# Sparse attention, a dense layer and routed experts on one core: the second batch's attention rearranged, the first weight transfer moved, sums scaled on another engine

## The chip, the cores and the metric

One core of one Trainium2 chip runs the whole program. The metric is the time of one execution in device microseconds (us); lower is better. The engines are TensorE (PE in the rows; PEld is its weight load), VectorE (DVE), ScalarE (ACT), GpSimd (POOL) and SyncE (SP), which here issues the transfers. Each engine runs its own list of instructions in a fixed order, and waits at an instruction until what it needs is there.

## What is computed

The reference, cut to what matters:

```python
# 4 batches, 8 heads, 576 positions, head size 64
scores = scale * q @ k^T            # heads 0-3: the last 32 positions; heads 4-7: every 32nd position
attn   = exp(scores - max);  attn = attn / (sum(attn) + 1e-9)
x      = attn @ v                   # 2304 tokens x 512
h      = x @ w_in                   # 512 -> 2048
g      = where(h >= 1, h, where(h <= -1, 0, (h + 1)**2 / 4))
x      = g @ w_out                  # 2048 -> 512, written to the output
# second layer: tokens with x @ w_skip > 0 go to one of 8 experts:
out    = x + gate * (relu(x @ w1[e]) @ w2[e])
```

## The kernel before

The 2304 tokens are cut into blocks of 512 (the last one 256). For each block the dense layer takes 16 steps. A step of `gemm1` (line 450) multiplies the tokens by 128 columns of `w_in` in 12 matmuls into the bank `ph`; VectorE and ScalarE make `g` of it in four instructions (lines 468 to 471: VectorE, ScalarE, VectorE, ScalarE), and GpSimd makes its low half. `gemm2` (line 475) runs three steps behind and adds 12 matmuls into the four banks `po`. Numbers are held as two fp16 halves (high and low), hence three products each.

The weights come as fp64 and are turned into fp16 halves by `load_w` (line 108): one transfer of 1 MB, six VectorE instructions (lines 128 to 130, twice) through the bank `tp`, two on ScalarE (134, 135), one on GpSimd (136). There are 16 such loads, i0 to i7 of `w_in` and o0 to o7 of `w_out`; their staging tiles have three buffers. Load i0 serves steps 0 and 1, o0 the second layer of the same steps, and so on.

Attention works on head pairs (`hp` 0 to 3) and two groups of tiles (`gi` 0 and 1). `scores` (line 191) writes the mask (line 196) and the products q k (line 204) into the bank `sc`. `softmax` (line 209) takes the maximum (220), the exponentials (by ScalarE for group 1, line 224; else 227 to 229), scales the sum (line 225 on ScalarE for group 1, line 230 on VectorE for group 0), takes the reciprocal (231), and GpSimd multiplies (232). `values` (line 236) multiplies by v into the bank `pv`, and `to_x` (line 254) writes the tokens `xr`, which `gemm1` reads. All attention instructions of batch b have to be done before the block that holds its tokens can run: block 1 needs batch 1.

Batch 0 has its own routine, `attention32` (line 276), which transposes on TensorE. The others use `attention` (line 325), which is a generator: head pair by head pair it splits v (`vn`, lines 336 to 341), scores both groups, turns the probabilities with a transposing transfer (`pT`, line 356, one buffer per group), and multiplies by v. For batch 1 the scores and the products with v share the one bank `sc`. `Filler` (line 519) hands out the generator's pieces between the steps: batch 1 over the first 13 steps, the weights over 13 steps, batch 2 over steps 16 to 25.

A scheduler then sets the order on each engine; `after(a, b)` only tells it that a stands behind b. Transfers are issued by SyncE in its order: those of batch 0 first (`load_qkv`, four head pairs), then the first weights.

Of the kernel before, what the change touches and what calls it, by code (L numbers as in the profile page):

```python
# [8 lines left out]
F32 = mybir.dt.float32  # L9
F16 = mybir.dt.float16  # L10
# [3 lines left out]
AF = mybir.ActivationFunctionType  # L14
ALU = mybir.AluOpType
# [5 lines left out]
def kernel(ctx: ExitStack, tc: tile.TileContext, q, k, v, w_in, w_out, w_skip, w_gate, w1, w2, out):  # L21
    nc = tc.nc
    B, S, D = 4, 576, 64
# [167 lines left out]
    def scores(b, hp, gi, qkv, sc):  # L191

        g0, g1 = GROUPS[gi]
        kw, mask = (96, mloc) if hp < 2 else (72, mstr)
        nt = g1 - g0
        nc.tensor.matmul(  # L196
            sc[:, : nt * kw], identb, mask[:, g0:g1, :].rearrange("p n c -> p (n c)"), start=True, stop=False
        )
        for n in range(g0, g1):
            k0 = n * (64 if hp < 2 else 72)  # L200
            t = n - g0
            for j in range(2):
                js = slice(j * D, (j + 1) * D)
                mm = nc.tensor.matmul(  # L204
                    sc[js, t * kw : (t + 1) * kw], qkv[0][js, n, :], qkv[1][js, k0 : k0 + kw], start=False, stop=n == g1 - 1
                )
        return mm

    def softmax(b, hp, gi, sc, by_act):

        g0, g1 = GROUPS[gi]
        kw = 96 if hp < 2 else 72
        nt = g1 - g0
        nm = f"{b}_{hp}_{gi}"
        scv = sc[:, : nt * kw].rearrange("p (n c) -> p n c", n=nt)
        sm = att.tile([P, nt, kw], F32, tag="sm", name=f"sm_{nm}", bufs=3)
        st = att.tile([P, 3, 5], F32, tag="st", name=f"st_{nm}", bufs=4)
        mx, su, ri = (st[:, e, :nt] for e in range(3))
        wide_k = lambda x: x.unsqueeze(2).to_broadcast([P, nt, kw])
        red = nc.vector.tensor_reduce(mx, scv, AX.X, ALU.max, negate=by_act)  # L220
        if by_act:
            nc.scalar.mul(mx, mx, SCL)
            for t in range(nt):
                nc.scalar.activation(sm[:, t], scv[:, t], AF.Exp, bias=mx[:, t : t + 1], scale=SCL, accum_out=su[:, t : t + 1])  # L224
            nc.scalar.activation(su, su, AF.Copy, bias=1.0e-9 / XS, scale=1.0 / XS)
        else:
            nc.vector.tensor_tensor(sm, scv, wide_k(mx), ALU.subtract)
            nc.scalar.activation(sm, sm, AF.Exp, scale=SCL)
            nc.vector.reduce_sum(su, sm, axis=AX.X)
            nc.vector.tensor_scalar(su, su, 1.0e-9, 1.0 / XS, ALU.add, ALU.mult)  # L230
        nc.vector.reciprocal(ri, su)  # L231
        nc.gpsimd.tensor_tensor(sm, sm, wide_k(ri), ALU.mult)  # L232
        marks["red", b, hp, gi] = red
        return sm
# [41 lines left out]
    def attention32(b):  # L276

        units = [(hp, gi) for hp in range(4) for gi in range(2)]
        held = {}

        def scored(hp, gi):
            i = 2 * hp + gi
            pool, tag = (ps_s, "sc") if i % 2 else (ps_v, "pv")
            sc = pool.tile([P, 512], F32, tag=tag, name=f"sc_{b}_{hp}_{gi}")
            held["mm"] = scores(b, hp, gi, held[hp], sc)
            held[hp, gi] = softmax(b, hp, gi, sc, gi == 1)

        def turned(hp, gi):
            g0, g1 = GROUPS[gi]
            kw = 96 if hp < 2 else 72  # L290
            sm = held[hp, gi]
            pT = att.tile([96, 5, P], F32, tag="pT", name=f"pT_{b}_{hp}_{gi}", bufs=2)
            for c0, c1, tag in ((0, 3, "po0"), (3, 5, "po1")) if gi == 0 else ((0, 4, "po2"),):
                pp = ps_o.tile([P, 512], F32, tag=tag, name=f"pp_{b}_{hp}_{gi}_{c0}")
                if c0 == 0:
                    keep_warm(16 if hp == 0 else 4, pp, held["mm"])
                for t in range(c0, c1):
                    nc.tensor.transpose(pp[:kw, (t - c0) * P : (t - c0 + 1) * P], sm[:, t], ident)  # L298
                nc.scalar.copy(pT[:kw, c0:c1], pp[:kw, : (c1 - c0) * P].rearrange("p (t r) -> p t r", r=P))
            held[hp, gi] = pT  # L300

        def valued(hp, gi):
            kw = 96 if hp < 2 else 72
            pv = ps_h.tile([P, 512], F32, tag="ph", name=f"pv_{b}_{hp}_{gi}")
            v32 = held[hp][2]

            def pairs(n, j):
                at = 0 if n < GROUPS[0][1] else 1
                return [(v32[:kw, n, j, :], held[hp, at][:kw, n - GROUPS[at][0], j * D : (j + 1) * D])]

            values(hp, gi, pv, pairs)
            to_x(pv, b, hp, gi, 1.0)

        for hp in range(4):
            held[hp] = load_qkv(b, hp)
        for i in range(len(units) + 2):
            if i >= 2:
                valued(*units[i - 2])
            if 1 <= i <= len(units):
                turned(*units[i - 1])  # L320
            if i < len(units):
                scored(*units[i])
            yield

    def attention(b):

        nxt = load_qkv(b, 0)
        for hp in range(4):
            kw = 96 if hp < 2 else 72
            nv = 96 if hp < 2 else 80  # L330
            qkv, nxt = nxt, load_qkv(b, hp + 1) if hp < 3 else None
            vn = att.tile([96, 2, NTL, 2, D], F16, tag="vn", name=f"vn_{b}_{hp}", bufs=1)
            v32 = qkv[2].rearrange("p n h d -> p (n h d)")
            vh, vl = (vn[:nv, e].rearrange("p n h d -> p (n h d)") for e in range(2))
            if b == 1:
                nc.scalar.activation(v32, v32, AF.Copy, scale=XS)
                nc.scalar.activation(vh, v32, AF.Copy)
                nc.gpsimd.tensor_tensor(vl, v32, vh, ALU.subtract)
            else:
                nc.scalar.activation(vh, v32, AF.Copy, scale=XS)  # L340
                nc.vector.scalar_tensor_tensor(vl, v32, XS, vh, ALU.mult, ALU.subtract)
            pTs = []
            yield
            for gi in range(2):
                g0, g1 = GROUPS[gi]
                nt = g1 - g0
                nm = f"{b}_{hp}_{gi}"
                sc = bank(f"sc_{nm}")
                scores(b, hp, gi, qkv, sc)
                sm = softmax(b, hp, gi, sc, gi == 1)  # L350
                pn = p_b[gi][:, : 2 * nt * P].rearrange("p (e t c) -> p e t c", e=2, t=nt)
                pnh, pnl = (pn[:, e, :, :kw] for e in range(2))
                nc.scalar.activation(pnh, sm, AF.Copy)  # L353
                nc.gpsimd.tensor_tensor(pnl, sm, pnh, ALU.subtract)  # L354
                pT = att.tile([P, 2, nt, P], F16, tag=f"pT{gi}", name=f"pT_{nm}", bufs=1)
                nc.sync.dma_start_transpose(pT.rearrange("p e t r -> p (e t) r"), pn.rearrange("p e t c -> p (e t c)"))
                pTs.append(pT)
                yield
            for gi in range(2):
                if b == 1:  # L360
                    pv = ps_s.tile([P, 512], F32, tag="sc", name=f"pv_{b}_{hp}_{gi}")
                else:
                    pv = ps_v.tile([P, 512], F32, tag="pv", name=f"pv_{b}_{hp}_{gi}")

                def pairs(n, j):
                    at = 0 if n < GROUPS[0][1] else 1
                    r = [pTs[at][:kw, e, n - GROUPS[at][0], j * D : (j + 1) * D] for e in range(2)]
                    l = [vn[:kw, e, n, j, :] for e in range(2)]
                    return [(l[0], r[0]), (l[0], r[1]), (l[1], r[0])]

                values(hp, gi, pv, pairs)
                to_x(pv, b, hp, gi, 1.0 / XS)
                yield

    def spread(t, x2):
# [74 lines left out]
    def gemm1(n, fs):  # L450
# [4 lines left out]
        for i, f in enumerate(fs):  # L455
            step = 0
            for cc in range(NCC):
                for we, xe in ((0, 0), (0, 1), (1, 0)):
                    nc.tensor.matmul(  # L459
                        ph[:, i * nt : (i + 1) * nt], w_in_s[:, we, cc, f * P : (f + 1) * P],  # L460
                        xr[:, xe, cc, t0 % XR : t0 % XR + nt], start=step == 0, stop=step == 11,
                    )
# [5 lines left out]
        nc.vector.tensor_scalar(uu, h, XS * WS, -XS * WS, ALU.min, ALU.max)  # L468
        nc.scalar.activation(uu, uu, AF.Square, bias=half, scale=0.5 * GS ** 0.5 / (XS * WS))  # L469
        nc.vector.scalar_tensor_tensor(uu, h, GS / (XS * WS), uu, ALU.mult, ALU.max)  # L470
        nc.scalar.activation(gh, uu, AF.Copy)  # L471
        nc.gpsimd.tensor_tensor(gl, uu, gh, ALU.subtract)  # L472
        gs[n, fs[0]] = g

# [64 lines left out]
            for f in fillers:  # L539
                f.upto(t + 1)  # L540

    NA = 4 * (1 + 2 * 2)
    att_b = [attention32(0)] + [attention(b) for b in range(1, B)]

    pairs_w = [("i", 0), ("i", 1)]
# [8 lines left out]
    marks["early"] = True  # L554
    keep_warm(48, ps_v.tile([P, 512], F32, tag="pv", name="idle"))
    for i, _ in enumerate(att_b[0]):
        if i >= 7 and i - 7 < 2:
            after(next(ws), marks["red", 0, 3, i - 7])
    marks["early"] = False
    next(ws)  # L560
    NW = 13
    fw = Filler(ws, NW, 0, NW)
    f1 = Filler(att_b[1], NA, 0, 13)
    f2 = Filler(att_b[2], NA, 16, 25)
    f3 = Filler(att_b[3], NA, 32, 45)
    wide[0] = False
# [301 lines left out]
```

## Time and profile before

| | us |
|---|---|
| three timed runs | 508.18, 506.29, 503.13; median 506.29 |
| the profiled execution: its time, and its span | 505.59, 503.8 |
| TensorE busy in the span | 463.7 |
| mean granted TensorE clock, share of full speed | 0.966 |

The span is from the first to the last instruction; 1.8 us lie around it. Busy time of TensorE counts overlapping matmuls once. A digit in the slices of the profile's page stands for 12.6 us.

### The profile page before, as it was taken

The page shows a single profiled execution, that of the slowest core. Times are in us where ns is not written, and L with a number is a line of the kernel's source. Part 1 is how long each engine was busy: PE and PEld are TensorE (multiplying, and loading weights), DVE is VectorE, ACT ScalarE, POOL GpSimd, SP SyncE. Part 2 cuts the span into 40 slices and gives each one's busy share as a digit, 9 for nine tenths or more (in the row PEclk, how much of TensorE's full clock was granted, in tenths as well). Part 3 has the DMA queues.
Part 4 walks back from the last instruction along what each step waited for, and adds up shares of the span by engine and source line. Part 5 has one row for each costly group of instructions (what it writes and reads, how often), then busy time and mean ns, then how long its engine had stood idle before and what let it go on. Part 6 is the DMA issues. An engine that isn't in the chain of part 4 may idle for free.

```text
span 503.8 us, 9766 instructions
## 1 busy us (share of the span) xinstructions
PE 463.7 (92%) x3836; PEld 246.3 (49%) x3836; DVE 282.2 (56%) x597; ACT 244.0 (48%) x505; POOL 198.6 (39%) x188
## 2 busy tenths in 40 slices
PE   8767899999965999999999999999999999989990
PEld 7653344444433545544445444544444444558750
DVE  4597999999333555436345553632363466565411
ACT  2674776766553655443236534342432355564210
POOL 4325577776620653421435323262113411121330
PEclk9978899999985999999999999999999999999997
DMA  8968777589157363440009112021250245635001
GB/s 226 313 206 267 238 195 243 154 256 269 29 132 191 81 135 73 94 105 1 2 21 194 27 23 47 1 44 26 66 103 1 85 168 167 174 120 128 2 2 50
DMA packets 69513, 58.72 MB, mean 117 GB/s; under 512 B 49226, under 2 KB 53322, under 8 KB 69456
## 3 DMA queue, kind: packets, MB, share of 16 engines
q1 hardware_dynamic: 68848, 57.96, 42.1%
q8 instruction: 32, 0.52, 0.4%
q14 instruction: 25, 0.20, 0.1%
q0 software_dynamic: 608, 0.03, 0.1%
HBM read 41.93 MB, written 5.03 MB: 93 GB/s over the span
## 4 chain that ended last, share of the span: by engine, by line
PE 74%; DMA 12%; DVE 6%; ACT 3%; SPq 1%; issue 1%; POOL 0%; POOLq 0%; DVEq 0%; ACTq 0%
PE ph L459 32%; PE po L483 32%; DMA esta<-in_moe_w_dram 5%; PE sc L204 3%; DMA v<-in_v_dram 3%; PE pv L252 3%; DMA k<-in_k_dram 2%; DMA pT<-p_b 1%; DVE w1sa L634 1%; ACT w1sa L633 1%; DVE w2sa L634 1%; PE sc L196 1%; PE eha L163 1%; PE pya L163 1%; PE pr L163 1%
## 5 line engine op out<-in xcount | busy, mean ns | idle before, releaser
L459 PE MATMUL ph<-xr,w_in_s 128*128 128x512 f16 (+1 forms) x960 | 206.2, 362 | 8.3 <-DVE uu L470 7.7
L483 PE MATMUL po<-w_out_s,g 128*128 128x512 f16 x864 | 201.0, 379 | 0.0
L472 POOL TENSOR_TENSOR g<-uu,g 128x512 f16<-128x512 f32 x72 | 84.5, 1174 | 168.4 <-ACT g L471 154.7
L459 PEld LDWEIGHTS <-w_in_s 128*128 128x128 f16 x960 | 91.9, 99 | 100.7 <-issue 11.4
L483 PEld LDWEIGHTS <-g 128*128 128x128 f16 x864 | 83.5, 98 | 97.3
L469 ACT ACTIVATE uu<-uu,half 128x512 f32<-128x512 f32 x72 | 51.7, 718 | 83.4 <-DVE uu L468 82.9
L468 DVE TENSOR_SCALAR uu<-ph 128x512 f32<-128x512 f32 x72 | 49.3, 685 | 49.0 <-PE ph L459 47.7
L470 DVE SCALAR_TENSOR_TENSOR uu<-ph,uu 128x512 f32<-128x512 f32 x72 | 49.5, 688 | 32.1 <-ACT uu L469 31.9
L471 ACT ACTIVATE g<-uu 128x512 f16<-128x512 f32 x72 | 45.1, 626 | 42.0 <-DVE uu L470 40.4
L232 POOL TENSOR_TENSOR sm<-sm,st 128x384 f32<-128x384 f32 (+3 forms) x32 | 26.2, 820 | 65.9 <-DVE st L231 49.6
L204 PE MATMUL sc<-k,q 64*64 64x96 f32 (+1 forms) x576 | 30.2, 246 | 3.0 <-DMA k<-in_k_dram 3.0
L204 PEld LDWEIGHTS sc<-k,q 64*64 64x64 f32 x576 | 24.2, 138 | 14.6 <-issue 14.0
L274 DVE SCALAR_TENSOR_TENSOR xr<-pv,xr 128x288 f16<-128x288 f32 (+5 forms) x38 | 15.1, 403 | 27.4 <-ACT xr L273 27.4
L220 DVE TENSOR_REDUCE st<-sc 128x5 f32<-128x480 f32 (+3 forms) x32 | 17.4, 546 | 21.0 <-PE sc L204 20.7
L354 POOL TENSOR_TENSOR p_b<-sm,p_b 128x480 f16<-128x480 f32 (+3 forms) x24 | 22.6, 941 | 14.6 <-ACT p_b L353 13.4
L273 ACT ACTIVATE xr<-pv 128x288 f16<-128x288 f32 (+5 forms) x38 | 13.8, 364 | 28.1 <-PE pv L252 27.2
L252 PE MATMUL pv<-pT,vn 96*64 96x64 f16 (+2 forms) x684 | 16.6, 200 | 9.8 <-DMA pT<-p_b 8.0
L252 PEld LDWEIGHTS <-vn 72*64 72x64 f16 (+1 forms) x684 | 13.7, 116 | 19.0 <-issue 17.2
L432 POOL DMA_INDIRECT lst<-ent,si x16 | 16.0, 997 | 14.9 <-DMA lst<-ent,si 13.4
L224 ACT ACTIVATE sm<-sc,st 128x96 f32<-128x96 f32 (+1 forms) x64 | 20.3, 330 | 2.6 <-PE pp L298 2.1
L136 POOL TENSOR_TENSOR w_in_s<-tvi,w_in_s 128x1024 f16<-128x1024 f32 x8 | 17.1, 2132 | 6.1 <-ACT w_in_s L135 4.3
L136 POOL TENSOR_TENSOR w_out_s<-tvo,w_out_s 128x1024 f16<-128x1024 f32 x8 | 17.1, 2133 | 4.0 <-ACT w_out_s L135 2.9
(141 smaller groups left out, 413.8 us busy)
## 6 DMA issues: line engine op xcount, KB each, us to landing
wi<-in_moe_w_in_dram SPq DMA_DIRECT2D x8, 1024.0 KB, 5.7
wo<-in_moe_w_out_dram SPq DMA_DIRECT2D x8, 1024.0 KB, 5.3
esta<-in_moe_w_dram SPq DMA_DIRECT2D x16, 512.0 KB, 3.6
q<-in_q_dram SPq DMA_DIRECT2D x16, 288.0 KB, 5.2
out_dram<-x SPq DMA_DIRECT2D x18, 256.0 KB, 2.1
v<-in_v_dram SPq DMA_DIRECT2D x8, 432.0 KB, 7.6
v<-in_v_dram SPq DMA_DIRECT2D x8, 360.0 KB, 6.6
k<-in_k_dram SPq DMA_DIRECT2D x8, 324.0 KB, 5.6
```

What stands on the lines that cost most here:

```text
L136: nc.gpsimd.tensor_tensor(dst[1], tvf, dst[0], ALU.subtract)
L204: mm = nc.tensor.matmul(sc[js, t * kw : (t + 1) * kw], qkv[0][js, n, :], qkv[1][js, k0 : k0 + kw], start=False, stop=n == g1 - 1)
L232: nc.gpsimd.tensor_tensor(sm, sm, wide_k(ri), ALU.mult)
L252: nc.tensor.matmul(oo, l, r, start=i == 0, stop=i == len(todo) - 1)
L354: nc.gpsimd.tensor_tensor(pnl, sm, pnh, ALU.subtract)
L459: nc.tensor.matmul(ph[:, i * nt : (i + 1) * nt], w_in_s[:, we, cc, f * P : (f + 1) * P], xr[:, xe, cc, t0 % XR : t0 % XR + nt], start=step ...
L468: nc.vector.tensor_scalar(uu, h, XS * WS, -XS * WS, ALU.min, ALU.max)
L469: nc.scalar.activation(uu, uu, AF.Square, bias=half, scale=0.5 * GS ** 0.5 / (XS * WS))
L470: nc.vector.scalar_tensor_tensor(uu, h, GS / (XS * WS), uu, ALU.mult, ALU.max)
L471: nc.scalar.activation(gh, uu, AF.Copy)
L472: nc.gpsimd.tensor_tensor(gl, uu, gh, ALU.subtract)
L483: nc.tensor.matmul(pos[n][s], g[:, ge, i * nt + s * P : i * nt + (s + 1) * P], w_out_s[:, we, f, :], start=f == 0 and si == 0, stop=f == N ...
```

## The change

The scaling of the sums, line 230 on VectorE, becomes an instruction on ScalarE for both groups. The four buffers of the transposed probabilities get one name and size for batch 0 and the others. In batch 0's routine the first weight load stands ahead of the loads of head pair 3. `attention` becomes a pipeline: the loads run two head pairs ahead, the scores of head pair i stand ahead of the products with v of head pair i-1, and v is split after them; `pT` has four buffers. For batch 1, the products with v of group 1 use the bank `pv`, in which the weights' `tp` also lies; the scores stand behind the last `gemm1` matmul issued so far, and the first scaling of v behind the last `g`. Batch 1 is handed out over the first 10 steps, in 22 pieces instead of 20.

```diff
@@ scores
-        nc.tensor.matmul(
+        m0 = nc.tensor.matmul(
             sc[:, : nt * kw], identb, mask[:, g0:g1, :].rearrange("p n c -> p (n c)"), start=True, stop=False
         )
+        if b == 1:
+            after(m0, marks["gm"])
@@ softmax
-            nc.scalar.activation(su, su, AF.Copy, bias=1.0e-9 / XS, scale=1.0 / XS)
         else:
             nc.vector.tensor_tensor(sm, scv, wide_k(mx), ALU.subtract)
             nc.scalar.activation(sm, sm, AF.Exp, scale=SCL)
             nc.vector.reduce_sum(su, sm, axis=AX.X)
-            nc.vector.tensor_scalar(su, su, 1.0e-9, 1.0 / XS, ALU.add, ALU.mult)
-        nc.vector.reciprocal(ri, su)
+        nc.scalar.activation(su, su, AF.Copy, bias=1.0e-9 / XS, scale=1.0 / XS)
+        marks["rec", b, hp, gi] = nc.vector.reciprocal(ri, su)
@@ attention32
-            pT = att.tile([96, 5, P], F32, tag="pT", name=f"pT_{b}_{hp}_{gi}", bufs=2)
+            pT = att.tile([P, 10 * P], F16, tag="pT", name=f"pT_{b}_{hp}_{gi}", bufs=4)
+            pT = pT.bitcast(F32).rearrange("p (t r) -> p t r", t=5)[:96]
         for hp in range(4):
+            if hp == 3:
+                first_w = next(ws)
             held[hp] = load_qkv(b, hp)
         for i in range(len(units) + 2):
+            if i == 6:
+                after(first_w, marks["red", b, 2, 1])
@@ attention
-        nxt = load_qkv(b, 0)
-        for hp in range(4):
+        held = []
+        for hp in range(2):
+            held.append(load_qkv(b, hp))
+            yield
+        parts, turned = {}, {}
+
+        def scored(hp, gi):
...
+            pT = att.tile([P, 10 * P], F16, tag="pT", name=f"pT_{nm}", bufs=4)[:, : 2 * nt * P]
...
+        def split(hp):
...
             if b == 1:
-                nc.scalar.activation(v32, v32, AF.Copy, scale=XS)
+                after(nc.scalar.activation(v32, v32, AF.Copy, scale=XS), marks["ga"])
...
+        def valued(hp, gi):
+            kw = 96 if hp < 2 else 72
+            if b == 1 and gi == 0:
+                pv = ps_s.tile([P, 512], F32, tag="sc", name=f"pv_{b}_{hp}_{gi}")
+            else:
+                pv = ps_v.tile([P, 512], F32, tag="pv", name=f"pv_{b}_{hp}_{gi}")
...
+        for i in range(5):
+            if i < 2:
+                held.append(load_qkv(b, i + 2))
+            if i < 4:
+                for gi in range(2):
+                    scored(i, gi)
+                    yield
+            if i > 0:
+                for gi in range(2):
+                    valued(i - 1, gi)
+                    yield
+            if i < 4:
+                split(i)
                 yield
@@ gemm1
-                    nc.tensor.matmul(
+                    marks["gm"] = nc.tensor.matmul(
...
-        nc.scalar.activation(gh, uu, AF.Copy)
+        marks["ga"] = nc.scalar.activation(gh, uu, AF.Copy)
@@ the whole
-    NA = 4 * (1 + 2 * 2)
+    NA = 2 + 4 * (1 + 2 * 2)
     for i, _ in enumerate(att_b[0]):
-        if i >= 7 and i - 7 < 2:
-            after(next(ws), marks["red", 0, 3, i - 7])
+        if i == 8:
+            after(next(ws), marks["rec", 0, 3, 1])
-    f1 = Filler(att_b[1], NA, 0, 13)
+    f1 = Filler(att_b[1], NA, 0, 10)
```

What it moves shows in the order of the instructions. In the rows below, `ph_0` is the bank of step 0, `uu_0` and `g_0` what is made of it, and names such as `sc_0_0_732` carry head pair and group; the last number only tells tiles apart.

ScalarE before, from the second weight load (`tvi_609`) to step 0's first instruction:

```order
L134 ACTIVATE tvi_609<-tvi_609 128x1024
L273 ACTIVATE xr<-pv_3_0_583 128x18x16
L135 ACTIVATE w_in_s<-tvi_609 128x4x256
L273 ACTIVATE xr<-pv_3_1_621 128x18x16
L336 ACTIVATE v_0_684<-v_0_684 96x1152
L337 ACTIVATE vn_0_694<-v_0_684 96x1152
L336 ACTIVATE v_1_690<-v_1_690 96x1152
L134 ACTIVATE tvo_636<-tvo_636 128x1024
L228 ACTIVATE sm_0_0_744<-sm_0_0_744 128x480
L135 ACTIVATE w_out_s<-tvo_636 128x1024
L469 ACTIVATE uu_0_661<-uu_0_661,half 128x512
```

ScalarE now, the same place:

```order
L134 ACTIVATE tvi_609<-tvi_609 128x1024
L135 ACTIVATE w_in_s<-tvi_609 128x4x256
L495 ACTIVATE uu_0_661<-uu_0_661,half 128x512
L497 ACTIVATE g_0_662<-uu_0_661 128x512
L495 ACTIVATE uu_1_707<-uu_1_707,half 128x512
L134 ACTIVATE tvo_636<-tvo_636 128x1024
L135 ACTIVATE w_out_s<-tvo_636 128x1024
L497 ACTIVATE g_1_708<-uu_1_707 128x512
```

The two instructions on batch 1's v (L336) that stood ahead of step 0 stand behind step 2 now.

TensorE before, from batch 0's last products with v to step 0:

```order
L252 MATMUL pv_3_0_583<-pT_3_0_534,v_3_210 64x16x4 x4
L252 MATMUL pv_3_1_621<-pT_3_1_596,v_3_210 64x16x4 x8
L204 MATMUL sc_0_0_732<-k_0_683,q_0_682 64x96 x10
L459 LDWEIGHTS w_in_s
L459 MATMUL ph_0_648<-xr,w_in_s 128x512
```

TensorE now, from step 1's last matmul to step 2:

```order
L485 MATMUL ph_1_694<-xr,w_in_s 128x512
L196 LDWEIGHTS identb
L196 MATMUL sc_0_0_734<-mloc,identb 128x480
L206 MATMUL sc_0_0_734<-k_0_683,q_0_682 64x96 x10
L485 LDWEIGHTS w_in_s
L485 MATMUL ph_2_784<-xr,w_in_s 128x512
```

Batch 1's first scores stood between batch 0's attention and step 0; they stand between steps 1 and 2 now.

VectorE before, at the end of the weights and the scores of batch 1's head pair 3 (`st_3_0`):

```order
L129 SCALAR_TENSOR_TENSOR tpo_1656<-wo_1649,tpo_1656 128x512
L468 TENSOR_SCALAR uu_14_1778<-ph_14_1765 128x512
L231 RECIPROCAL st_2_1_1345<-st_2_1_1345 128x4
L130 SCALAR_TENSOR_TENSOR tvo_1651<-wo_1649,tpo_1656 128x512
L470 SCALAR_TENSOR_TENSOR uu_14_1778<-ph_14_1765,uu_14_1778 128x512
L468 TENSOR_SCALAR uu_15_1810<-ph_15_1797 128x512
L274 SCALAR_TENSOR_TENSOR xr<-pv_2_0_1405,xr 128x18x16
L470 SCALAR_TENSOR_TENSOR uu_15_1810<-ph_15_1797,uu_15_1810 128x512
L274 SCALAR_TENSOR_TENSOR xr<-pv_2_1_1438,xr 128x18x16
L220 TENSOR_REDUCE st_3_0_1580<-sc_3_0_1567 128x5
```

VectorE now, at the scores of the same head pair:

```order
L275 SCALAR_TENSOR_TENSOR xr<-pv_1_0_1134,xr 128x320
L275 SCALAR_TENSOR_TENSOR xr<-pv_1_1_1236,xr 128x256
L222 TENSOR_REDUCE st_3_0_1326<-sc_3_0_1313 128x5
L128 TENSOR_SCALAR tpo_1302<-wo_1299 128x512
L228 TENSOR_TENSOR sm_3_0_1325<-sc_3_0_1313,st_3_0_1326 128x360
L129 SCALAR_TENSOR_TENSOR tpo_1302<-wo_1299,tpo_1302 128x512
L230 TENSOR_REDUCE st_3_0_1326<-sm_3_0_1325 128x5
L130 SCALAR_TENSOR_TENSOR tvo_1301<-wo_1299,tpo_1302 128x512
L232 RECIPROCAL st_3_0_1326<-st_3_0_1326 128x5
L128 TENSOR_SCALAR tpo_1306<-wo_1299 128x512
L494 TENSOR_SCALAR uu_10_1604<-ph_10_1591 128x512
```

Head pair 3's scores stood behind the last weight load and step 15; they stand inside the load of o4 and ahead of step 10 now.

## Rows read from the trace of the kernel before

**Rows 1.** The profile's page: busy time by engine; TensorE and its clock, 40 slices.
```profile
PE 463.7 (92%) x3836; PEld 246.3 (49%) x3836; DVE 282.2 (56%) x597; ACT 244.0 (48%) x505; POOL 198.6 (39%) x188
...
PE   8767899999965999999999999999999999989990
...
PEclk9978899999985999999999999999999999999997
```

**Rows 2.** Who TensorE waited for, first 170 us: total, times, longest.
```profile
PE pv L252 <- DMA pT<-p_b: 8.0, 2, 4.8
PE ph L459 <- DVE uu L470: 5.2, 2, 5.0
```

**Rows 3.** Timeline of TensorE, 18 to 68 us: start, length, idle before and its end.
```profile
19.39 0.34 PE L204 MATMUL sc<-k,q 64*64 64x72 f32 x4 [0.44 <-DMA k<-in_k_dram]
...
38.74 1.86 PE L204 MATMUL sc<-k,q 64*64 64x96 f32 x20 [1.72 <-DMA k<-in_k_dram]
40.54 6.40 PE L459 MATMUL ph<-xr,w_in_s 128*128 128x512 f16 x24
...
52.87 4.44 PE L459 MATMUL ph<-xr,w_in_s 128*128 128x512 f16 x12 [4.97 <-DVE uu L470]
```

**Rows 4.** Timeline of ScalarE, the same stretch.
```profile
40.70 1.16 ACT L336 ACTIVATE v<-v 96x1152 f32<-96x1152 f32 x1 [2.52 <-DMA v<-in_v_dram]
...
44.53 1.16 ACT L336 ACTIVATE v<-v 96x1152 f32<-96x1152 f32 x1 [1.47 <-DMA v<-in_v_dram]
45.60 1.04 ACT L134 ACTIVATE tvo<-tvo 128x1024 f32<-128x1024 f32 x1
```

**Rows 5.** Timeline of VectorE: first weights, batch 0's end, step 0, the last weights.
```profile
24.83 0.68 DVE L128 TENSOR_SCALAR tpi<-wi 128x512 int32<-128x512 int32 x1
...
38.56 0.45 DVE L274 SCALAR_TENSOR_TENSOR xr<-pv,xr 128x288 f16<-128x288 f32 x1
...
48.33 1.97 DVE L230 TENSOR_SCALAR st<-st 128x5 f32<-128x5 f32 x1
50.22 0.68 DVE L468 TENSOR_SCALAR uu<-ph 128x512 f32<-128x512 f32 x1
...
127.19 0.66 DVE L130 SCALAR_TENSOR_TENSOR tvo<-wo,tpo 128x512 int32<-128x512 int32 x1
```

**Rows 6.** Timeline of GpSimd at 48 us.
```profile
48.16 2.12 POOL L136 TENSOR_TENSOR w_out_s<-tvo,w_out_s 128x1024 f16<-128x1024 f32 x1 [2.65 <-ACT w_out_s L135]
```

**Rows 7.** Timeline of TensorE, 128 to 172 us.
```profile
145.70 0.72 PE L204 MATMUL sc<-k,q 64*64 64x72 f32 x16
151.21 1.02 PE L252 MATMUL pv<-pT,vn 72*64 72x32 f16 x30 [4.79 <-DMA pT<-p_b]
...
157.47 0.86 PE L252 MATMUL pv<-pT,vn 72*64 72x64 f16 x24 [3.17 <-DMA pT<-p_b]
...
163.40 2.75 PE L459 MATMUL ph<-xr,w_in_s 128*128 128x512 f16 x12 [0.27 <-DVE uu L470]
```

**Rows 8.** Chain that ended last, in order of time, 55 to 105 us: start, length, what.
```profile
57.31 2.59 PE po L483 x12
...
79.77 0.97 PE sc L204 x20
...
99.83 0.60 PE pv L252 x30
```

**Rows 9.** Stretches: length, then each engine's busy us (instructions); clock, DMA share, GB/s.
```profile
15.00:20.00 5.00, 3.54 (x61) 2.72 (x58) 2.16 (x7) 3.00 (x13) 1.76 (x3) 1.00 1.05 257
```

**Rows 10.** Stretches of 10 us, the same columns.
```profile
110.00:120.00 10.00, 10.00 (x78) 4.93 (x75) 9.79 (x17) 6.10 (x8) 8.11 (x5) 1.00 1.01 317
130.00:140.00 10.00, 10.00 (x75) 4.70 (x74) 2.07 (x4) 3.73 (x6) 6.76 (x5) 1.00 0.14 28
```

**Rows 11.** Lines 225 and 230: count, ns min/median/max, first and last start.
```profile
L225 ACT ACTIVATE st<-st x16: 191/208/231, 11.9 to 331.2; 128x4 f32<-128x4 f32 x16
...
L230 DVE TENSOR_SCALAR st<-st x16: 138/159/1974, 12.8 to 325.6; 128x5 f32<-128x5 f32 x16
```

More of the change, by code (lines that the diff above doesn't have):

```diff
@@ L325, in attention @@
     def attention(b):
-        nxt = load_qkv(b, 0)
-        for hp in range(4):
-            kw = 96 if hp < 2 else 72
+        held = []
[4 more added lines that the diff above has]
+        def scored(hp, gi):
+            g0, g1 = GROUPS[gi]
+            nt = g1 - g0
+            kw = 96 if hp < 2 else 72
+            nm = f"{b}_{hp}_{gi}"
+            sc = bank(f"sc_{nm}")
+            scores(b, hp, gi, held[hp], sc)
+            sm = softmax(b, hp, gi, sc, gi == 1)
+            pn = p_b[gi][:, : 2 * nt * P].rearrange("p (e t c) -> p e t c", e=2, t=nt)
+            pnh, pnl = (pn[:, e, :, :kw] for e in range(2))
+            nc.scalar.activation(pnh, sm, AF.Copy)
+            nc.gpsimd.tensor_tensor(pnl, sm, pnh, ALU.subtract)
+            pT = att.tile([P, 10 * P], F16, tag="pT", name=f"pT_{nm}", bufs=4)[:, : 2 * nt * P]
+            pT = pT.rearrange("p (e t r) -> p e t r", e=2, t=nt)
+            nc.sync.dma_start_transpose(pT.rearrange("p e t r -> p (e t) r"), pn.rearrange("p e t c -> p (e t c)"))
+            turned[hp, gi] = pT
+        def split(hp):
             nv = 96 if hp < 2 else 80
-            qkv, nxt = nxt, load_qkv(b, hp + 1) if hp < 3 else None
             vn = att.tile([96, 2, NTL, 2, D], F16, tag="vn", name=f"vn_{b}_{hp}", bufs=1)
-            v32 = qkv[2].rearrange("p n h d -> p (n h d)")
+            v32 = held[hp][2].rearrange("p n h d -> p (n h d)")
             vh, vl = (vn[:nv, e].rearrange("p n h d -> p (n h d)") for e in range(2))
             if b == 1:
-                nc.scalar.activation(v32, v32, AF.Copy, scale=XS)
+                after(nc.scalar.activation(v32, v32, AF.Copy, scale=XS), marks["ga"])
                 nc.scalar.activation(vh, v32, AF.Copy)
@@ L341, in attention @@
                 nc.vector.scalar_tensor_tensor(vl, v32, XS, vh, ALU.mult, ALU.subtract)
[L342 to L372, printed above, removed]
+            parts[hp] = vn
@@ new lines, in valued, with pairs @@
+        def valued(hp, gi):
[4 more added lines that the diff above has]
+                pv = ps_v.tile([P, 512], F32, tag="pv", name=f"pv_{b}_{hp}_{gi}")
+            def pairs(n, j):
+                at = 0 if n < GROUPS[0][1] else 1
+                r = [turned[hp, at][:kw, e, n - GROUPS[at][0], j * D : (j + 1) * D] for e in range(2)]
+                l = [parts[hp][:kw, e, n, j, :] for e in range(2)]
+                return [(l[0], r[0]), (l[0], r[1]), (l[1], r[0])]
+            values(hp, gi, pv, pairs)
+            to_x(pv, b, hp, gi, 1.0 / XS)
```

## The prediction

> **What bounds the kernel now.** I read the page first: TensorE is busy for 92% of the span, and its slices are at 9 but for the first five, a dip at slices 12 to 14 and the end [rows 1]. So TensorE is the bound nearly everywhere, and a change can gain only in those dips. The clock shows the same places, 7 and 8 in slices 3 and 4 and 6 in slice 13. A slice is 12.6 us, so the first dip lies before 60 us and the second near 150 us. The change touches both. The dip at the end belongs to the routed experts, which it leaves alone.
>
> Then the waits of TensorE, up to 170 us: two waits for `pT`, 8.0 us in all, and one of 5.0 us for VectorE's `uu` [rows 2]. The timelines say what these are.
>
> *First dip.* Step 0 starts at 40.54 us, after 1.72 us of waiting for k of batch 1, whose scores stand ahead of it [rows 3]. Its 24 matmuls with step 1 take 6.40 us where 24 at full clock take 5.18 (two groups of 12 at 2.59) [rows 3, 8]. Then TensorE stands for 4.97 us until 52.87, and the next 12 take 4.44 us, that is 1.85 us more than at full clock [rows 3]. The chain behind that wait runs through ScalarE: it waited for two transfers of batch 1's v and was through with the second scaling only at 45.6 [rows 4]. Behind it stood o0's conversion, the exponential of batch 1 and step 0. VectorE's first `uu` came at 50.22, just after a scaling of five sums that took 1.97 us [rows 5].
>
> *Second dip.* Batch 1's last scores end at 146.4 us, its last products wait twice for `pT`, and TensorE is back at its work at 163.40 [rows 7]. Block 1 cannot go on without that head pair. From 57 to 146 us TensorE never waits, while VectorE is at 9.79 of 10 us in a stretch such as 110 to 120 and then falls to 2.07 in 130 to 140 [rows 10]: the weights were done, and the last head pair had not been let in.
>
> **The change part by part.**
>
> *The first weights ahead of head pair 3* move 1 MB ahead of q, k and v of that pair (0.97 MB). At 257 GB/s [rows 9] i0 lands some 4 us earlier and k of pair 3 some 4 us later. TensorE met that k at 19.39 with a wait of 0.44 us [rows 3]; it will meet it near 23.4. VectorE can begin i0 near 21 where it began at 24.83 [rows 5], so most of the 19 weight and softmax instructions that lay mixed between 24.8 and 38.6 are gone from the path of pair 3. I walked that path with the durations of before: from k at 23.4 through scores, softmax, transposes and products, last `xr` near 39, as before (39.0, from 38.56 and 0.45 [rows 5]). The first nine matmuls of step 0 don't need pair 3, and batch 1's scores no longer stand ahead. I take step 0 at 37.2 instead of 40.54. The bounds are 34 (k no later than now) and 41.5 (the full 4 us passed on to pair 3).
>
> *The v scaling behind `g`, the scores behind steps 0 and 1.* The waits of 2.52 and 1.47 us on ScalarE [rows 4] go, and with them TensorE's 4.97 us. Next to be late is VectorE: step 0's `uu`, the rest of i1 and o0, step 1's `uu`, 13 instructions at 0.6 us. By that, steps 0 and 1 end at 43.6 (6.40 again, since TensorE idles before), the scores at 44.8, steps 2 and 3 by 50.3, then two groups of `gemm2` and two sets of scores: 57.5. Before, TensorE at 57.3 had done steps 0 to 2 and two sets of scores. It is ahead by three groups of 2.59 and one set of scores, 1.1 with its mask (0.97 in [rows 8]): 8.9, less 0.2 for the clock times, **8.7 us** gained.
>
> *The pipeline and the 10 steps* let the last head pair in beside o4. If it ends before block 1 asks for it, the stretch from 146.4 to 163.40 shrinks to its work: 60 products (1.2), six matmuls of steps 0 and 1 of block 1 (1.3), one set of scores with its mask (1.2) [rows 8]. That is 17.0 - 3.7 = **13.3 us** gained, the slow clock after the wait included (30 products took 1.02 us at 151.21 [rows 7] and 0.60 elsewhere [rows 8]).
>
> *What it costs: VectorE.* From step 0's first `uu` to the last weight instruction VectorE has 125 instructions before and 153 now, counted in the order: 82 of weights for 74, 32 of steps for 29, 39 others for 22. The 125 took from 50.22 to 127.85, 0.62 us each [rows 5]. At that rate 153 take 95.0 us, from about 41.5 to 136.5. ScalarE (two of 1.04 [rows 4]) and GpSimd (2.12 [rows 6]) come behind, so o7 is whole at 140.7. TensorE without waits would ask for it at 57.5 + 26 groups of 2.59 (67.3) + 11.0 of attention = 135.8. So VectorE is late by some 5 us at the end, where before it was early. On the way I find i2 late by 2.5 us, i6 by 5 and i7 by 2, for these loads come in heaps behind the scores. The bounds are 0 (VectorE has gaps to fill: what it waits for now comes earlier) and 16 (95.0 - 77.6 = 17.4 of added VectorE work on the path, less its slack of 5, plus twice 1.85 us of slow clock). I take **8 us**, nearest to the walk.
>
> *The sums on ScalarE.* 16 instructions of 159 ns median leave VectorE and come to ScalarE at 208 ns [rows 11]; ScalarE is at 6.10 of 10 us [rows 10] and hides 0.2 us each. On VectorE the worst took 1.97 us [rows 5] while GpSimd ran one from 48.16 to 50.28 [rows 6]. With four of them in batch 1 VectorE gets back between 0.6 and 7.9 us; this is inside the rate of 0.62 us and therefore in the bounds of the 8 us, and I add nothing. If ScalarE were full, each would delay a reciprocal by one ScalarE instruction, about 1 us.
>
> The Trainium skill, "SBUF — State Buffer", section "Who interferes with whom", says that VectorE and GpSimd share a port pair as an exclusive lock, which `tensor_scalar` from SBUF to SBUF can take, but also a VectorE instruction with two SBUF inputs against a GpSimd one that reads SBUF. The first half agrees with the 1.97 us; the second speaks against the change, since batch 2's split of v (two SBUF inputs, VectorE) is now drawn in between the weights of o6, beside GpSimd's 2.12 us. By that rule one such wait of up to 2.1 us is added to VectorE; no row of before shows it, and the sum leaves it out.
>
> *More `pT` buffers, loads two pairs ahead.* Cost nothing: SyncE's list holds the same transfers, and no VectorE instruction waited for a weight transfer in this trace. In batches 2 and 3 TensorE is at 9 [rows 1] and hides what changes there.
>
> *Sum.* The profiled execution's 505.6 - 8.7 - 13.3 + 8 = **491.6**, say 491.5. That execution lies 0.7 us under the median of 506.3, inside the 5 us that the three runs spread, so I keep it for both. About 1% of the time, 5 us, is what a measurement here can tell from no change.
>
> **The rivals.**
>
> *TensorE alone sets the time.* For it: from 57 to 146 us it never waited though VectorE was full. Against: VectorE gets 28 instructions more in the same work. No loss: 505.6 - 22.0 = 483.5.
>
> *The start gains nothing and VectorE costs most.* k of pair 3 comes 4 us late and the path takes it over, the weights are late throughout: 505.6 - 4 - 13.3 + 12 = 500.
>
> *The last head pair is late all the same.* It doesn't do what it says: products of group 1 wait for `tp`, the dip at 146 stays. Only the start is gained: 505.6 - 8.7 = 497. Against: its scores stand five steps further ahead.
>
> *Slower: the shared bank.* Each product of group 1 of batch 1 needs the bank of `tp`, and the next weight instruction on VectorE needs it back, after TensorE, ScalarE and VectorE have used it. Where TensorE comes to it two groups late, VectorE stands for 5.2 us with all weights and `uu` behind it, four times: 21 us more. 505.6 - 22.0 + 8 + 21 = 512.5. It decides from a lag of some 3.5 us each time (14 us for the four, all that the forecast gains). Against: the order puts these products where VectorE's work of about the same length lies between, by my walk they meet within 2 us.
>
> **How the numbers follow.** The forecast 0.50, TensorE alone 0.18, the start without gain 0.17, the late head pair 0.07, slower 0.08. Faster by over 1% (under 500.5): the first two, the late pair, and half of the third: 0.83. Within 1%: the other half and a little of the slower case, 0.10. Slower: 0.07. The range reaches from below the second case to the third: 481 to 501.
>
> **What would show it.** Right: step 0 near 37 us; no wait of 5 us after step 1, but small ones before steps 4, 12 and 14, for GpSimd's low half of the weights; VectorE full until about 137 us; no dip at 146 to 163, and TensorE at block 1's step 2 near 150. The waits for `pT` gone. Wrong: step 0 after 41 us; waits of TensorE over 16 us in 57 to 150; VectorE idle for several us in front of a weight instruction (the shared bank); or batch 1's last `xr` after 140 us.

## The result, and the profile after

The changed kernel takes 500.12 us (median of 20 runs, 497.08 to 506.14), the kernel before 505.92 us (20 runs): a ratio of 0.987, 95% interval [0.985, 0.9892]. It is faster by 5.8 us by these medians, where 14 were forecast. The ratio is taken without two slow runs of the changed kernel, 504.81 and 506.14 us. The time lies inside the forecast range, near its upper end. The profiled execution has a span of 498.5 us (before 503.8).

The page of the kernel after, busy time and the slices of TensorE and its clock, for [rows 1]:

```profile
PE 464.4 (93%) x3836; PEld 244.8 (49%) x3836; DVE 278.5 (56%) x581; ACT 245.4 (49%) x521; POOL 197.7 (40%) x188
...
PE   8589799978899999999999999999999999989992
...
PEclk9899999999789999999999999999999999999997
```

The clock dip of slices 3 and 4 is gone (a digit of 8 in slice 2 is new), and so is TensorE's dip at 139 to 163 us. In their place TensorE's slices 9 to 11 have fallen to 7 and 8, and the clock has a new dip in slices 11 and 12, at 125 to 150 us. Who TensorE waited for in the first 170 us, for [rows 2] (total, times, longest):

```profile
PE po L509 <- ACT w_out_s L135: 4.6, 3, 2.1
PE sc L206 <- DMA k<-in_k_dram: 3.5, 2, 3.1
PE sc L196 <- ACT sm L226: 3.0, 3, 1.8
PE ph L485 <- POOL w_in_s L136: 2.3, 2, 1.2
PE ph L485 <- ACT w_in_s L135: 1.9, 2, 1.2
```

The waits for `pT` and the 5 us for `uu` are not there any more. TensorE now waits for weights. Its timeline shows where, for [rows 3, 7]:

```profile
37.67 5.34 PE L485 MATMUL ph<-xr,w_in_s 128*128 128x512 f16 x24
...
57.49 0.36 PE L196 MATMUL sc<-mloc,identb 128*128 128x480 bf16 x1 [1.76 <-ACT sm L226]
...
107.80 1.02 PE L509 MATMUL po<-w_out_s,g 128*128 128x512 f16 x4 [1.71 <-ACT w_out_s L135]
...
125.46 1.87 PE L509 MATMUL po<-w_out_s,g 128*128 128x512 f16 x4 [2.08 <-ACT w_out_s L135]
127.66 6.18 PE L509 MATMUL po<-w_out_s,g 128*128 128x512 f16 x20 [0.34 <-POOL w_out_s L136]
...
136.06 1.04 PE L485 MATMUL ph<-xr,w_in_s 128*128 128x512 f16 x4 [1.24 <-ACT w_in_s L135]
138.26 6.01 PE L485 MATMUL ph<-xr,w_in_s 128*128 128x512 f16 x20 [1.17 <-POOL w_in_s L136]
```

Step 0 starts at 37.67, near the forecast 37.2, and its 24 matmuls with step 1 run at full clock: 5.34 us, where the forecast had 6.40. The third set of scores, forecast to be done at 57.5, begins at 57.49, after a wait of 1.76 us for ScalarE's exponentials. Behind it come many waits of 0.3 to 2.1 us, all small. Twenty matmuls take 6.2 and 6.0 us at 127.66 and 138.26, against 4.49 at full clock (at 110.31, for one). What stood behind these waits is on VectorE (its timeline, after):

```profile
98.77 0.42 DVE L275 SCALAR_TENSOR_TENSOR xr<-pv,xr 128x256 f16<-128x256 f32 x1 [3.40 <-ACT xr L274]
...
115.89 0.46 DVE L275 SCALAR_TENSOR_TENSOR xr<-pv,xr 128x288 f16<-128x288 f32 x1 [4.13 <-ACT xr L274]
116.39 0.69 DVE L128 TENSOR_SCALAR tpo<-wo 128x512 int32<-128x512 int32 x1
...
124.50 0.46 DVE L275 SCALAR_TENSOR_TENSOR xr<-pv,xr 128x288 f16<-128x288 f32 x1 [1.07 <-ACT xr L274]
...
134.00 1.35 DVE L367 SCALAR_TENSOR_TENSOR vn<-v,vn 96x1152 f16<-96x1152 f32 x1 [3.15 <-ACT vn L366]
...
147.43 0.67 DVE L130 SCALAR_TENSOR_TENSOR tvo<-wo,tpo 128x512 int32<-128x512 int32 x1
```

VectorE stands three times in front of `xr` of group 1, whose bank is that of `tp`, with the next weight instruction behind it (after the second wait it is the one at 116.39, L128, `tpo`). This is the sign that the prediction had named for the shared bank. The last weight instruction, forecast for 136.5 us, comes at 147.43. From step 0's first `uu` to that instruction VectorE stands for 16.9 us in all: 8.6 in these three waits, 3.2 for batch 2's v (at 134.00), the rest mostly for `ph` and for ScalarE's `uu`. Before, it stood for 1.4 us between the same two instructions. ScalarE's timeline shows what the second of the three waits hung on, and another wait:

```profile
115.45 0.41 ACT L274 ACTIVATE xr<-pv 128x288 f16<-128x288 f32 x1 [1.69 <-PE pv L253]
...
132.80 1.16 ACT L366 ACTIVATE vn<-v 96x1152 f16<-96x1152 f32 x1 [7.39 <-DMA v<-in_v_dram]
```

The first of the three hung on two engines: TensorE's products of group 1 end at 96.83, but ScalarE comes to their `xr` only at 98.37, behind two weight instructions. At 115 us the three engines waited in a ring: TensorE had come to these products only after 20 matmuls of `gemm2` that themselves had waited for `w_out_s` at 107.80; ScalarE waited for the products, VectorE for ScalarE, and the weights that TensorE wants at 125.46 lay behind VectorE.

The size of the loss is read from the stretch of 57 to 139 us. First the kernel before, then the one after, with 120 to 145 us too (length, then busy us of TensorE, its weight load, VectorE, ScalarE, GpSimd; clock, DMA share, GB/s):

```profile
57.00:139.00 82.00, 82.00 (x587) 38.95 (x586) 70.98 (x118) 55.98 (x97) 58.76 (x41) 1.00 0.68 197
```

```profile
57.00:139.00 82.00, 70.26 (x609) 33.58 (x609) 65.37 (x113) 53.81 (x106) 54.39 (x40) 0.95 0.67 193
120.00:145.00 25.00, 19.32 (x150) 8.40 (x149) 18.61 (x30) 11.10 (x16) 8.92 (x6) 0.80 0.76 224
```

TensorE lost 11.7 us to waits. At a clock of 0.80 the 19.3 busy us of 120 to 145 did the work of 15.5, which is 3.9 us more (an estimate, since it takes the mean clock of the stretch for the busy time). Together 15.6 us; the two forecast gains of 22.0 less the measured 5.8 leave 16.2. VectorE is not fuller than before, it is emptier: 65.37 us for 70.98.

### The profile page after: what moved, and what is told of

It is laid out like the page before. It is cut to its first block, busy times and chain, and to the rows that moved or that the text cites. A ratio compares the mean times of both kernels' runs of the same rounds, so it can differ in the third digit from the quotient of the medians.

```text
span 498.5 us, 9753 instructions
## 1 busy us (share of the span) xinstructions
PE 464.4 (93%) x3836; PEld 244.8 (49%) x3836; DVE 278.5 (56%) x581; ACT 245.4 (49%) x521; POOL 197.7 (40%) x188
## 4 chain that ended last, share of the span: by engine, by line
PE 66%; DMA 13%; DVE 9%; ACT 6%; issue 2%; SPq 1%; POOL 1%; DVEq 0%; ACTq 0%
PE po L509 29%; PE ph L485 28%; DMA esta<-in_moe_w_dram 5%; PE pv L253 3%; PE sc L206 3%; DMA k<-in_k_dram 3%; DMA v<-in_v_dram 2%; DMA xsT<-xs 1%; DMA q<-in_q_dram 1%; DVE uu L496 1%; DVE w1sa L660 1%; DVE uu L494 1%; DVE tpo L129 1%; DVE tpo L128 1%; DVE w2sa L660 1%
## 5 line engine op out<-in xcount | busy, mean ns | idle before, releaser
L485 PE MATMUL ph<-xr,w_in_s 128*128 128x512 f16 (+1 forms) x960 | 203.9, 360 | 7.5 <-DVE uu L496 3.0
L485 PEld LDWEIGHTS <-w_in_s 128*128 128x128 f16 x960 | 90.7, 98 | 98.1 <-issue 4.1
L206 PE MATMUL sc<-k,q 64*64 64x96 f32 (+1 forms) x576 | 28.7, 239 | 3.5 <-DMA k<-in_k_dram 3.5
L206 PEld LDWEIGHTS sc<-k,q 64*64 64x64 f32 x576 | 22.9, 133 | 17.3 <-issue 17.1
L136 POOL TENSOR_TENSOR w_in_s<-tvi,w_in_s 128x1024 f16<-128x1024 f32 x8 | 17.0, 2130 | 27.8 <-ACT w_in_s L135 19.3
```

The costliest lines, as they stand in the source:

```text
L136: nc.gpsimd.tensor_tensor(dst[1], tvf, dst[0], ALU.subtract)
L206: mm = nc.tensor.matmul(sc[js, t * kw : (t + 1) * kw], qkv[0][js, n, :], qkv[1][js, k0 : k0 + kw], start=False, stop=n == g1 - 1)
L485: marks["gm"] = nc.tensor.matmul(ph[:, i * nt : (i + 1) * nt], w_in_s[:, we, cc, f * P : (f + 1) * P], xr[:, xe, cc, t0 % XR : t0 % XR + n ...
```

## The experiments

All times are medians, each with its ratio to the kernel before, run beside it (505.3 to 505.8 us). The edits are to the changed kernel, but for the last.

| edit | us | ratio, 95% interval |
|---|---|---|
| batch 1's products in one bank | 490.8 | 0.9713 [0.9637, 0.979] |
| batch 1 over 13 steps | 491.34 | 0.9711 [0.9642, 0.9781] |
| both | 489.46 | 0.9679 [0.9631, 0.9727] |
| batch 2's first split behind the weights | 500.77 | 0.9899 [0.983, 0.9969] |
| the same, and one bank | 491.85 | 0.9723 [0.9668, 0.9778] |
| first weights behind head pair 3 | 505.49 | 0.9979 [0.9941, 1.0017] |
| group 0's sums on VectorE, all batches | 511.6 | 1.012 [1.0062, 1.0178] |
| the same, batch 0 alone | 505.28 | 1.0001 [0.9962, 1.0041] |
| the same, batch 1 alone | 506.69 | 1.0012 [0.9977, 1.0048] |
| sums on VectorE, one bank, 13 steps | 496.36 | 0.9837 [0.9799, 0.9875] |
| kernel before, sums on ScalarE | 503.88 | 0.9973 [0.9939, 1.0007] |

**One bank for batch 1's products.**

```diff
-            if b == 1 and gi == 0:
+            if b == 1:
```

> The changed kernel, but batch 1's products with v of both groups use the bank of the scores, none the bank of the weights' tp. Theory (shared bank: VectorE stands 3.4 and 4.1 us before the xr of group 1, with the next weight instructions behind it): these waits go and the time falls by 2 to 4 us, to 496 to 498. Rival (VectorE stands there because TensorE or ScalarE comes late to the products, in whatever bank): the waits stay, and the scores of the next head pair come later too, since one bank holds them all: 500 to 506.

490.8 us, 9.3 under the changed kernel, more than twice what the theory had. VectorE's timeline and two stretches:

```profile
121.70 0.68 DVE L130 SCALAR_TENSOR_TENSOR tvo<-wo,tpo 128x512 int32<-128x512 int32 x1
...
130.26 0.46 DVE L275 SCALAR_TENSOR_TENSOR xr<-pv,xr 128x288 f16<-128x288 f32 x1 [2.19 <-ACT xr L274]
```

```profile
57.00:139.00 82.00, 80.42 (x592) 37.94 (x589) 68.33 (x116) 59.15 (x110) 57.91 (x42) 1.00 0.70 196
139.00:170.00 31.00, 27.84 (x273) 14.86 (x274) 17.19 (x29) 16.19 (x35) 12.44 (x12) 0.89 0.45 108
```

The last weight instruction comes at 121.70 instead of 147.43, TensorE is back at 80.42 of 82 us, and the wait for `xr` comes after the weights, where no weight instruction stands behind it any more. Part of the price shows at 139 to 170, a small dip (27.84 of 31 us) where batch 1's last products come late. So in this order the bank that products and weights share costs the 9 us.

**13 steps instead of 10, with the bank shared.**

```diff
-    f1 = Filler(att_b[1], NA, 0, 10)
+    f1 = Filler(att_b[1], NA, 0, 13)
```

> The changed kernel, but batch 1 is handed out over the first 13 steps instead of 10. Theory (weights and attention come in heaps: 13 us of short waits of TensorE between 56 and 139 us come from squeezing both): with the same work over more steps these waits sum to 6 to 9 us and the time is 495 to 498. Rival (the waits come from the total of VectorE's work, which is the same): they sum to 12 to 14 us and the time is 499 to 501; a wait for the last head pair returns before block 1 if the 10 steps were needed, then 503 or more.

491.34 us, as good as the one bank, and less than the theory's 495. The last weight instruction (VectorE's timeline) is at 137.56. No `xr` of batch 1 is waited for ahead of it; the one wait stands before head pair 3's two `xr`, behind the weights:

```profile
137.56 0.69 DVE L130 SCALAR_TENSOR_TENSOR tvo<-wo,tpo 128x512 int32<-128x512 int32 x1
...
141.15 0.93 DVE L275 SCALAR_TENSOR_TENSOR xr<-pv,xr 128x288 f16<-128x288 f32 x2 [2.91 <-ACT xr L274]
```

**Both.**

> Batch 1 with both edits: its sums in one bank as before, and over 13 steps. Theory (one loss: the shared bank makes TensorE, ScalarE and VectorE wait for each other only where attention is squeezed, so each undoing removes the same loss): 488 to 492, within 2 us of the two single ones (490.8 and 491.3). Rival (two separate losses of 9 us each, VectorE's load and the bank): they add, 480 to 484.

489.46 us, within 2 us of either alone: they don't add. The loss is one, the shared bank in a stretch too dense for it. This is the lowest time of the kernels run; its interval lies under that of the changed kernel, but not apart from those of the two single edits.

**Batch 2's first split of v behind the last weights,** against ScalarE's wait of 7.39 us.

```diff
-                nc.scalar.activation(vh, v32, AF.Copy, scale=XS)
-                nc.vector.scalar_tensor_tensor(vl, v32, XS, vh, ALU.mult, ALU.subtract)
+                va = nc.scalar.activation(vh, v32, AF.Copy, scale=XS); b == 2 and hp == 0 and after(va, marks["wa"])
+                vv = nc.vector.scalar_tensor_tensor(vl, v32, XS, vh, ALU.mult, ALU.subtract); b == 2 and hp == 0 and after(vv, marks["wv"])
```

> The changed kernel, but batch 2's first split of v stands behind the last weight instruction on ScalarE and on VectorE. Theory (ScalarE's wait of 7.4 us for batch 2's v at 125 to 133 us holds up the conversion of i7 and o6): that wait goes, step 14 starts at about 135 instead of 136 to 138 us and at full clock, and the kernel takes 3 to 5 us less than the changed one, 495 to 497. Rival (VectorE's added work is what is late, whatever ScalarE does): the wait goes, but the time stays within 1 us of the changed kernel's 500.

500.77 us, no gain: one of five runs took 495.66, the others 499.93 to 502.3, and the profile is of that one. The 7.39 us are gone in it, but one wait for the shared bank grew from 4.13 to 5.71 us (VectorE's timeline):

```profile
116.05 0.46 DVE L275 SCALAR_TENSOR_TENSOR xr<-pv,xr 128x288 f16<-128x288 f32 x1 [5.71 <-ACT xr L274]
```

> One bank for batch 1's sums, and batch 2's first split of v behind the last weights. Theory (ScalarE's 7.4 us wait for batch 2's v costs the path some 2 us, hidden in the first experiment by the waits for the shared bank): 487.5 to 489.5, 1.5 to 3 us under 490.8. Rival (the wait lies beside the slow clock and TensorE's queue and costs nothing): 490 to 492.

With one bank the same edit gives 491.85 against 490.8 without it: again no gain. The rival's figure holds: this wait, the longest single one of the dense steps, costs nothing that shows. With four runs each, spread over 489.9 to 493.4 and 488.6 to 494.3 us, a gain of 1 us or so can't be excluded.

**First weights behind head pair 3, as before.**

```diff
-            if hp == 3:
-                first_w = next(ws)
             held[hp] = load_qkv(b, hp)
+        first_w = next(ws)
```

> The changed kernel, but the first weight transfer stands behind those of batch 0's head pair 3, as before. Theory (the early weights bring step 0 from 40.5 to 37.7 us by themselves): step 0 starts 2 to 3 us later and the time is 502 to 503. Rival (step 0 comes early because batch 1's scores and v no longer stand ahead of it): step 0 starts at 37 to 38 us all the same, the wait of 3.1 us for k at 21.6 us is gone, and the time is 499 to 500.5.

505.49 us: 5.4 us slower than the changed kernel, more than the theory's figure. Two stretches of this kernel, and step 0 and the same scores as above on TensorE's timeline:

```profile
0.00:37.00 37.00, 29.37 (x396) 23.94 (x396) 19.38 (x51) 18.34 (x67) 13.87 (x31) 0.83 0.91 272
37.00:57.00 20.00, 20.00 (x144) 10.61 (x141) 16.31 (x29) 10.87 (x17) 7.23 (x5) 0.80 0.71 226
```

```profile
41.25 7.12 PE L484 MATMUL ph<-xr,w_in_s 128*128 128x512 f16 x24
...
62.85 0.36 PE L196 MATMUL sc<-mloc,identb 128*128 128x480 bf16 x1 [1.76 <-ACT sm L226]
```

The scores stand at 62.85 against 57.49, 5.4 us later. Of this 3.6 are step 0's later start (41.25 against 37.67), and 1.8 are the clock: the 24 matmuls of steps 0 and 1 take 7.12 us for 5.34, and the clock of 37 to 57 us is 0.80, where in the changed kernel it is 1.00.

**Group 0's sums on VectorE again.** First for all batches, then for one batch alone (`if by_act or not (b == 0)`, and `b == 1`).

```diff
-        nc.scalar.activation(su, su, AF.Copy, bias=1.0e-9 / XS, scale=1.0 / XS)
+        if by_act:
+            nc.scalar.activation(su, su, AF.Copy, bias=1.0e-9 / XS, scale=1.0 / XS)
+        else:
+            nc.vector.tensor_scalar(su, su, 1.0e-9, 1.0 / XS, ALU.add, ALU.mult)
```

> The changed kernel with group 0's sums scaled on VectorE again (both batches' order otherwise kept). Theory (that edit is worth nothing, as VectorE was not full where TensorE waited): within 1.5 us of 500.1. Rival (it frees VectorE in the dense steps): 502 or more.

511.6 us, slower than before the change: the edit that I had thought worth nothing carries 11.5 us.

> The changed kernel with only batch 0's four group 0 sums scaled on VectorE. In the run with all of them there, step 0 came 0.4 us later and was cut in two by batch 0's last sums, some 3 us lost before 57 us. Theory (the 11.5 us are lost in both places, about 3 in batch 0): 502 to 504.5. Rival (all of it comes from batch 0's order, which shifts what follows): 509 to 512.

> The changed kernel with only batch 1's four group 0 sums scaled on VectorE. Theory (losses in both places): 506 to 509, as some 8 us lie here, in the dense steps with the shared bank. Rival (all from batch 0): within 1.5 us of 500.1.

505.28 and 506.69 us, 5.2 and 6.6 us over the changed kernel. The sum of 11.8 is the 11.5 of both at once. So neither rival holds: the loss lies in both places, with batch 0's part larger than the 3 us of the theory. In the profile with batch 0's sums on VectorE, the third set of scores begins at 61.23, 3.7 us later than in the changed kernel; the rest comes behind it. Of batch 1's four scalings (L234 in this kernel) the last three were long. VectorE's and GpSimd's timelines, batch 1 alone on VectorE:

```profile
63.86 1.98 DVE L234 TENSOR_SCALAR st<-st 128x5 f32<-128x5 f32 x1
...
86.09 1.17 DVE L234 TENSOR_SCALAR st<-st 128x5 f32<-128x5 f32 x1
...
105.35 2.32 DVE L234 TENSOR_SCALAR st<-st 128x5 f32<-128x5 f32 x1
```

```profile
62.81 2.13 POOL L136 TENSOR_TENSOR w_out_s<-tvo,w_out_s 128x1024 f16<-128x1024 f32 x1
64.89 0.92 POOL L353 TENSOR_TENSOR p_b<-sm,p_b 128x384 f16<-128x384 f32 x1
...
84.86 2.37 POOL L367 TENSOR_TENSOR vn<-v,vn 96x1152 f16<-96x1152 f32 x1
...
105.28 2.36 POOL L367 TENSOR_TENSOR vn<-v,vn 80x1152 f16<-80x1152 f32 x1 [1.45 <-ACT vn L366]
```

They end at 65.84, 87.26 and 107.67; the GpSimd instructions beside them end at 65.81, 87.23 and 107.64. These scalings of five numbers were through when GpSimd was, the first only behind two GpSimd instructions in a row: 5.5 us on VectorE for three. The Trainium skill, "SBUF — State Buffer", section "Who interferes with whom", says that `tensor_scalar` can take the port pair which VectorE shares with GpSimd, and that whoever issues second is then blocked for the whole instruction of the other. These rows agree.

> One bank and 13 steps (489.5), and the group 0 sums on VectorE in all batches. Theory (where the dense steps have room, only batch 0's part of some 3 us is left): 491.5 to 494.5. Rival (the edit is worth its 11 us wherever it stands): 499 to 502.

496.36 us, 6.9 above the same kernel with the sums on ScalarE. This lies between the two expectations: with room, some of the 11.5 us stays away, but more is left than batch 0's part was thought to be.

**The kernel before, with the sums on ScalarE and nothing else.** The diff is the `softmax` part of the change's, without the mark at the reciprocal.

> The kernel before with nothing changed but group 0's sums on ScalarE. Theory (worth something only with the early first weights and the dense steps of the change): 503 to 507, no change that can be measured against 505.8. Rival (worth its 11 us by itself): 494 to 497.

503.88 us, 1.4 under before with an interval that reaches to no change. TensorE's wait of 4.97 us for `uu` is 3.69 us there. The edit is worth little in the old order, and much in the new one.

## Why the prediction was right, and where wrong

*The first dip, 8.7 us: right in the main, the match at 57.5 us in part by luck.* Step 0 stands at 37.67 (37.2 forecast). Steps 0 and 1 took 5.34 us at full clock, where the prediction had carried the 6.40 over from before; the wait of 1.76 us for the exponentials, which it hadn't seen, takes that back. The three sets of scores that it had done at 57.5 are done at 58.8, so by its own count 7.4 us are gained. Undoing the early weights alone costs 5.4. These are the stretches of 37 to 57 us before and after:

```profile
37.00:57.00 20.00, 13.31 (x75) 6.55 (x74) 16.19 (x26) 12.44 (x21) 10.67 (x7) 0.77 0.77 243
```

```profile
37.00:57.00 20.00, 18.62 (x126) 9.14 (x127) 19.72 (x35) 14.86 (x27) 12.04 (x8) 1.00 0.81 264
```

*The second dip, 13.3 us: it went as forecast.* TensorE is at 31.00 of 31 us in the stretch of 139 to 170 us of the kernel after, where before it was at 20.55. Busy time times clock is 29.8 and 16.0, so 13.7 us of work at full speed were gained there (an estimate like the one above). These are the two rows:

```profile
139.00:170.00 31.00, 20.55 (x195) 11.10 (x193) 13.17 (x25) 13.69 (x31) 7.68 (x9) 0.78 0.52 134
```

```profile
139.00:170.00 31.00, 31.00 (x169) 14.21 (x167) 16.66 (x30) 18.72 (x39) 14.68 (x12) 0.96 0.43 113
```

*What it costs, 8 us: here the forecast failed.* The term was 16, twice the size, at the bound that I had set for it. I had counted VectorE's instructions at 0.62 us each and taken its load as the reason. The rate was right where VectorE doesn't stand: in the one-bank kernel the 138 instructions up to the last weight take 0.61 us each, with 0.5 us of standing. What the sum lacked was the 16.9 us in which VectorE stood. Half of it is the mechanism of the slower rival, the shared bank, at part of its price: VectorE stood 3.40 and 4.13 us, and 1.07 more at 124.50, in front of `xr` of group 1 with the weights behind it. That is 8.6 us, and one bank gives back 9.3. The rival had put 5.2 us four times. The step that failed is the sentence "by my walk they meet within 2 us": I dismissed the rival as a whole on it, and put none of its price into the likeliest case.

Two times agree with forecasts without bearing them out. The one-bank kernel's 490.8 is about what I had forecast for the kernel as it stood, but its weights end at 122 us, not near 136.5; most of what it still loses lies at 139 to 170. And the changed kernel's 500.12 is the 500 of the rival in which the start gains nothing, while the start did gain.

*The slow clock* at 120 to 145 us, 3.9 us, stood only in the upper bound, as "twice 1.85 us". It came behind TensorE's waits. In the one-bank kernel the clock was 1.00 from 57 to 139, and lower (0.89) only at 139 to 170, again behind waits.

*The sums on ScalarE, 0: no part of the error, but badly reasoned.* The bounds for VectorE in batch 1, 0.6 to 7.9 us, held the three long scalings, and the edit's 6.6 us there. I took it for covered by the rate of 0.62 us. In this order it decides between faster and slower than before.

*The port rule I weighed against the change.* Batch 2's split on VectorE took 1.35 us at 134.00, and the eight of its kind 1344 to 1355 ns; no wait of the 2.1 us came, and leaving it out of the sum was right. The one at 134.00 had no GpSimd instruction beside it. In the profile of the run with this split behind the last weights it had one, and took 2.33 us, 0.98 more (VectorE's and GpSimd's timelines):

```profile
143.90 2.33 DVE L367 SCALAR_TENSOR_TENSOR vn<-v,vn 96x1152 f16<-96x1152 f32 x1 [1.31 <-ACT vn L366]
```

```profile
142.89 2.13 POOL L136 TENSOR_TENSOR w_out_s<-tvo,w_out_s 128x1024 f16<-128x1024 f32 x1 [0.43 <-ACT w_out_s L135]
```

So this trace agrees, in one instruction, with the second half of the rule that the prediction takes from the Trainium skill.

*Readings.* TensorE's second dip before is slices 12 and 13 rather than 12 to 14, and the clock in slice 13 reads 5, not 6. Nothing in the sum rests on these digits.

*Still open.* Whether batch 0's 5.2 us come from a long scaling (the worst took 1.35 us) or from the order that the scheduler makes around it wasn't separated. In that profile step 0 is split: nine of its matmuls (3.79 us) stand at 38.17, ahead of batch 0's last products at 41.89. A bank of its own for `tp` wasn't tried; all eight banks that the kernel allocates are in use.

## What to carry to other kernels

When a change lets two kinds of work share a buffer, look in each engine's list for what stands right behind the instruction that hands it back. If it is the work that another engine will want next, a lag of a few us on one engine becomes a wait on all. A load summed at a mean duration says nothing of that, and spreading the work over more steps can cure it as well as a second buffer. A tiny instruction is not a cheap one: read its longest duration, and what ran beside it.

## What was not expected of the hardware

A scaling of 128x5 numbers on VectorE took 0.15 us, or up to 2.32 us when GpSimd was at work; three of batch 1's four ended within 0.03 us behind a GpSimd instruction. That this moves a kernel of 500 us by 6.6 us, from four such instructions, had not been expected. Nor had it been that a wait of 7.39 us of ScalarE, longer than any of TensorE's in these steps, would give back nothing that can be measured when it was taken away.
